# Linear attention and a gated feed-forward layer: the second tile's early work is queued behind the first x, and TensorE gets products of no use in the first attention's pauses

## The chip, the cores and the metric

The kernel runs on one core of one Trainium2 chip. A core has a matrix engine (TensorE, PE in the profile; PEld is its weight load), a vector engine (VectorE, DVE), a scalar engine (ScalarE, ACT), a general engine (GpSimd, POOL) and a queue that issues DMAs (SyncE, SP). They run side by side and wait for each other through semaphores; each takes its own instructions in order. The metric is the device time of one execution in microseconds; smaller is better.

## The reference

```
q_s = softmax of q over head_dim;  k_s = softmax of k over the sequence
kv  = k_s^T v                 # per batch and head, 64 x 64
x   = q_s kv                  # 8 batches x 576 tokens, 8 heads x 64 -> 4608 x 512
out = ((x @ w_a) * (x @ w_b)) @ w_out      # 512 -> 1536 -> 512
```

The weights w_a, w_b and w_out arrive as 64-bit floats; the kernel loads their words and makes 32-bit floats of them itself. Most products are made from a rounded operand ("hi") and its rest ("lo") in three passes.

## The kernel before, in words

The 4608 tokens are taken in nine tiles of 512. For every tile the attention makes x (four pairs of heads, g = 0 to 3), and the feed-forward runs over twelve blocks of 128 hidden columns, f = 0 to 11. Tile 0 uses plain products: `gate_first(f)` makes 24 products of 128 x 512 (two gates, four g, three passes each), `project_first(f)` four products in full float, two instructions each. The order on TensorE is gate 0, gate 1, projection 0, gate 2, projection 1, and so on. Tiles 1 to 8 use seven products per pair of blocks instead of eight (Strassen's scheme, operands B11, T2, T3, T1 and so on), and there TensorE is full.

Tile 0 is also the time in which the weights are made ready. `load_f(f)` loads two blocks of the gate weights (`raw`) and one of the output weights (`wo_raw`), 512 KB each. `convert_f(f)` (lines 517 to 520) rebuilds floats for each of the three in `to_float`: two copies on ScalarE (L97, L98), a shift on VectorE (L100), an addition on GpSimd (L101), a merge on VectorE (L102). For the two gate halves `convert_ab` then stores the floats (`dy`), splits them into hi and lo (`ws`: ScalarE L77, VectorE L80) and stores some of these (`dw`). `raw` tiles and the x tiles share one set of 11 buffers (tag `xo`).

The first attention (lines 525 to 540) runs, for each g: maximum and exponential of k (L236, L237), five transposes of it (L241), copies back (L242, L243), softmax of q (`q_soft_first` for even g, with sixteen small ScalarE instructions at L285; `q_soft` for odd g), the kv product (L249), its scaling and split (L254 to L257, L79, L80), four transposes of q (L316), their split (`qh`, `ql`), six or three x products (L333), and the split of x into hi and lo (L77, L80). `convert_f(0)` is traced after g = 1, `convert_f(1)` after g = 3.

In the loop over f that follows (lines 550 to 564), loads of later blocks, `convert_f(f + 2)`, one step of the second tile's attention (`attend()`, from f = 1 on: ten steps made of `s0` loads, `s1` softmax, `s2` products), the gate of f and the projection of f - 1 are traced in this order. `attention_tasks(1)` covers batch 1's four kv products and tile 1's four q.

The order in which the code is traced isn't the order of the queues: a planner at build time (line 685) orders each engine's instructions by an estimated timeline and takes up work early where an engine would be free and the buffers are there. `tc.issue_after(ins)` keeps the instructions of its block that run on `ins`'s engine behind `ins` in that engine's queue; it adds no wait between engines. Instructions of the block on other engines are not bound, DMA issues included.

Of the kernel before, what the change touches and what calls it, by code (L numbers as in the profile page):

```python
# [1 line left out]

# [5 lines left out]
F32 = mybir.dt.float32  # L8
# [5 lines left out]
ALU = mybir.AluOpType  # L14
# [15 lines left out]
def linear_attention_then_gated_ffn(  # L30
# [17 lines left out]
    nc = tc.nc  # L48
    B, NP, P, J, _, D = k.shape
# [3 lines left out]
    NF = 2 * NI  # L53
# [7 lines left out]
    ps = ctx.enter_context(tc.tile_pool(name="ps", bufs=1, space=bass.MemoryType.PSUM))  # L61
    dr = ctx.enter_context(tc.tile_pool(name="dr", bufs=1, space=bass.MemoryType.DRAM))

    ident = const.tile([P, P], F32, name="ident")
# [4 lines left out]
    mask = const.tile([P, P], F32, name="mask")  # L69
# [4 lines left out]
    def split(hi, lo, src, hi_engine="act"):  # L74

        if hi_engine == "act":
            nc.scalar.copy(out=hi, in_=src)  # L77
        else:
            nc.vector.tensor_copy(out=hi, in_=src)  # L79
        nc.vector.tensor_tensor(out=lo, in0=src, in1=hi.bitcast(F32), op=ALU.subtract)  # L80


    wo = {}
# [1 line left out]
    def to_float(raw):  # L85

        top = raw.bitcast(F32).rearrange("p (n t) -> p n t", t=2)[:, :, 1]
        low = raw.bitcast(U32).rearrange("p (n t) -> p n t", t=2)[:, :, 0]
        y = sb.tile([P, DM], F32, name="wy", bufs=8)
        r = sb.tile([P, DM], I32, name="wr", bufs=4)
        u = raw.bitcast(I32)[:, 0:DM]
        nc.scalar.activation(out=y, in_=top, func=AF.Copy, scale=2.0 ** -112)  # L97
        nc.scalar.activation(out=r, in_=low, func=AF.Copy, scale=2.0 ** -29)  # L98
        yi = y.bitcast(I32)
        nc.vector.tensor_single_scalar(u, yi, 3, op=ALU.logical_shift_left)  # L100
        nc.gpsimd.tensor_tensor(out=r, in0=u, in1=r, op=ALU.add)  # L101
        nc.vector.scalar_tensor_tensor(  # L102
            out=yi, in0=yi, scalar=-(2 ** 31), in1=r, op0=ALU.bitwise_and, op1=ALU.bitwise_or
        )
        return y
# [16 lines left out]
    def convert_wo(f):  # L122

        y = to_float(raws.pop((f, "o")))
        w = const.tile([P, 2, DM], F32R, name=f"wo{f}_w", tag=f"wo{f}")
        nc.sync.dma_start(out=w[:, 1].bitcast(F32), in_=y)
        wo[f] = w

    def split_wo(f):
        split(wo[f][:, 0], wo[f][:, 1], wo[f][:, 1].bitcast(F32))  # L130


    def ws_tile():
        return sb.tile([P, 2, 2, 2, P], F32R, name="ws", bufs=8)

    def split_w(y):
        w = ws_tile()
        yv = y.rearrange("p (n c f) -> p n c f", n=2, c=2)
        split(w[:, :, 0], w[:, :, 1], yv)
        return w  # L140

    dw, dy = {}, {}
    blocks = {}
# [1 line left out]
    def convert_ab(f, half):  # L145

        i, r = divmod(f, 2)
        y = to_float(raws.pop((f, half)))
        dy[i, r, half] = dr.tile([P, DM], F32, name=f"dy{i}{r}{half}")
        nc.sync.dma_start(out=dy[i, r, half], in_=y)  # L150
        w = split_w(y)
        op = ((A11, A12), (None, A22))[r][half]
        if op is not None:
            put_w(i, op, w)
        blocks[f, half] = w

    def put_w(i, op, w):
        dw[i, op] = dr.tile([P, 2, 2, 2, P], F32R, name=f"dw{i}{op}")
        nc.sync.dma_start(out=dw[i, op].bitcast(F32), in_=w.bitcast(F32))
# [30 lines left out]
    def v_load(b, g, vt=None):  # L190
        if vt is None:
            vt = sb.tile([P, J, 2, D + 1], F32, name="vt")
        nc.sync.dma_start(out=vt, in_=v[b, g])
        return vt
# [37 lines left out]
    def kv_soft_t(kt, tags):  # L232

        kf = kt.rearrange("p j c -> p (j c)")
        mc = sb.tile([P, 1], F32, name="mc")
        nc.vector.tensor_reduce(out=mc, in_=kf, axis=AX.X, op=ALU.max, negate=True)  # L236
        nc.scalar.activation(out=kf, in_=kf, func=AF.Exp, bias=mc)  # L237
        pa = ps.tile([P, J - 1, P], F32, name="pka", tag=tags[0])
        pb = ps.tile([P, P], F32, name="pkb", tag=tags[1])
        for j in range(J):  # L240
            nc.tensor.transpose(pa[:, j] if j < J - 1 else pb, kt[:, j], ident)  # L241
        nc.scalar.copy(out=kt[:, 0:J - 1], in_=pa)  # L242
        nc.vector.tensor_copy(out=kt[:, J - 1], in_=pb)  # L243
        return kt.rearrange("p j (h d) -> p j h d", h=2)

    def kv_product(kt, vt, tag="at"):
        pk = ps.tile([P, 2, D + 1], F32, name="pk", tag=tag)
        for j in range(J):
            nc.tensor.matmul(  # L249
                pk, kt[:, j].rearrange("p h d -> p (h d)"), vt[:, j],  # L250
                start=(j == 0), stop=(j == J - 1),
            )
        den = sb.tile([P, 1], F32, name="den")
        nc.vector.tensor_scalar_add(den, pk[:, 0, D:D + 1], EPS)  # L254
        nc.vector.reciprocal(out=den, in_=den)
        kv = sb.tile([P, P], F32, name="kv", bufs=1)
        nc.vector.scalar_tensor_tensor(  # L257
            out=kv.rearrange("p (h d) -> p h d", h=2), in0=pk[:, :, 0:D], scalar=den,
            in1=mask.rearrange("p (h d) -> p h d", h=2), op0=ALU.mult, op1=ALU.mult,
        )  # L260
        return kv
# [3 lines left out]
    def kv_split(b, g, kv):  # L265
        kvh = sb.tile([P, P], F32R, name=f"kvh{g}")
        kvl = sb.tile([P, P], F32R, name=f"kvl{g}")
        split(kvh, kvl, kv, "dve")
        kvs[b, g] = (kvh, kvl)
# [43 lines left out]
    def q_transpose(qt, tag="at"):  # L313
        pq = ps.tile([P, T], F32, name="pq", tag=tag)
        for j in range(TT):
            nc.tensor.transpose(  # L316
                pq[:, j * P:(j + 1) * P], qt[:, j].rearrange("p h d -> p (h d)"), ident
            )
        qh = sb.tile([P, T], F32R, name="qh", bufs=1)
        ql = sb.tile([P, T], F32R, name="ql", bufs=1)  # L320
        split(qh, ql, pq)
        return qh, ql

    def x_product(c, g, qhl, tag="at"):
        qh, ql = qhl
        t0 = c * T
        b0, b1 = t0 // S, (t0 + T - 1) // S
        n0 = min(T, (b0 + 1) * S - t0)
        px = ps.tile([P, T], F32, name="px", tag=tag)
        for b, s in ((b0, slice(0, n0)), (b1, slice(n0, T)))[:b1 - b0 + 1]:  # L330
            kvh, kvl = kvs[b, g]
            for i, (w, m) in enumerate(((kvh, qh), (kvh, ql), (kvl, qh))):
                nc.tensor.matmul(px[:, s], w, m[:, s], start=(i == 0), stop=(i == 2))  # L333
        return px


    def xo_tile(shape):
        return sb.tile(shape, F32R, name="xo", bufs=11)
# [168 lines left out]
    for g in range(NP):  # L507
        kt = const.tile([P, J, P], F32, name=f"kt_first{g}", tag=f"wo{NF - 1 - g}")
        vt = const.tile([P, J, 2, D + 1], F32, name=f"vt_first{g}", tag=f"wo{NF - 5 - g}")
# [3 lines left out]
        q_load(0, g, qt)  # L513
        v_load(0, g, vt)
    x0 = []

    def convert_f(f):
        convert_ab(f, 0)
        convert_ab(f, 1)
        convert_wo(f)  # L520

    for f in range(2):
# [2 lines left out]
    for g in range(NP):  # L525
        kt, vt, qt = first[g]
        odd = g % 2
        kt = kv_soft_t(kt, (("at", "k0"), ("k1", "k2"))[odd])
        if odd:
            q_soft(qt, True)  # L530
        else:
            q_soft_first(qt)
        kv_split(0, g, kv_product(kt, vt, ("po0", "po1")[odd]))
        qhl = q_transpose(qt, ("at", "k1")[odd])
        px = x_product(0, g, qhl, ("po2", "po3")[odd])
        x = xo_tile([P, 2, T])
        split(x[:, 0], x[:, 1], px)
        x0.append(x)
        if odd:
            convert_f(g // 2)  # L540


    early = (B11, T2, T3, T1)
# [2 lines left out]
    sy = {}  # L546
    attend = Spread(attention_tasks(1), 10)
    po = [ps.tile([P, DM], F32, name=f"po{t}") for t in range(TT)]
    pending = None
    for f in range(NF):  # L550
        for n in range(2, 4) if f == 0 else (f + 3,):
            if n < NF:
                last_load = load_f(n)
        if f + 2 < NF:
            convert_f(f + 2)
        if f:
            attend()
        if f == NF - 1:
            sy[0] = sums(0)
            x_operands(xfs[1], early + late, xo)  # L560
        ghl = gate_first(f, x0)
        if pending is not None:
            project_first(*pending, po)
        pending = (f, ghl)
# [11 lines left out]
    for c in range(1, NCH):  # L576
        more = c + 1 < NCH
        attend = Spread(attention_tasks(c + 1) if more else [], 3 * NI - 3)
        po = None
        x, xo = xo, {}  # L580
        for i in range(NI):
            def operand(op):
                if c > 1:
                    return get_w(i, op)
                if op in (A11, A12, A22):
                    return get_w(i, op)
                w = split_w(sy[i][op])
                put_w(i, op, w)
                return w

# [98 lines left out]
```

## Time and profile before

| | |
|---|---|
| median of 3 runs | 996.82 us (996.42 to 997.51) |
| the profiled execution | 995.74 us, of which span 993.3 us |
| busy: PE, DVE, ACT, POOL | 962.1, 654.0, 333.5, 114.2 us |
| mean granted clock of TensorE | 0.991 |

The span runs from the first to the last instruction; what is left of the profiled execution's time lies around it. All times in the rows below are counted from the span's start. A row of the timeline has the start, the duration, the engine, the line of the code, the instruction, what it writes and reads, how many were merged, and in brackets the idle time ahead of it and what ended it. Busy shares are averages over stages with different limits: tile 0, with its attention and conversions, takes the first 170 us or so, and the eight other tiles the rest.

### The profile page before, as it was taken

How to read it: one execution, taken by the hardware profiler on the slowest of the kernel's cores; microseconds unless marked ns; L12 is line 12 of the kernel's file. 1: busy time of each engine (PE TensorE's matmuls, PEld its weight loads, DVE VectorE, ACT ScalarE, POOL GpSimd, SP SyncE). 2: the span in 40 equal slices, each digit the busy share in tenths (PEclk: the TensorE clock that was granted, in tenths of full speed). 3: DMA queues.
4: the chain of work that ended last, by engine and by line, in shares of the span. 5: the costliest groups of instructions: out<-in, count | busy, mean ns of one | idle time of the engine just before them, and what ended most of it. 6: DMA issues, size and time to landing. Idle time of an engine off the chain costs nothing.

```text
span 993.3 us, 16580 instructions
## 1 busy us (share of the span) xinstructions
PE 962.1 (97%) x6276; PEld 866.0 (87%) x6276; DVE 654.0 (66%) x1280; ACT 333.5 (34%) x667; POOL 114.2 (11%) x96
## 2 busy tenths in 40 slices
PE   4889999999999999999999999999999999999998
PEld 4667666999989999999999999999999999999996
DVE  7797887887787774677468656865577555353433
ACT  7666675332342322233223212322233232121111
POOL 3344345440000000000000000000000000000000
PEclk9799998999999999999999999999999999999999
DMA  9599858978777587866796679767867676767761
GB/s 345 216 413 401 336 213 282 384 276 294 239 272 270 212 292 270 292 220 240 239 331 228 229 249 325 257 219 245 296 221 250 211 274 216 251 238 271 252 207 50
DMA packets 84605, 261.35 MB, mean 263 GB/s; under 512 B 9392, under 2 KB 9520, under 8 KB 84528
## 3 DMA queue, kind: packets, MB, share of 16 engines
q1 hardware_dynamic: 84528, 260.31, 73.8%
q8 instruction: 50, 0.82, 0.3%
q14 instruction: 27, 0.22, 0.1%
HBM read 219.38 MB, written 37.75 MB: 259 GB/s over the span
## 4 chain that ended last, share of the span: by engine, by line
PE 83%; DVE 4%; DMA 4%; issue 3%; ACT 2%; POOL 2%; SPq 0%; POOLq 0%; DVEq 0%; ACTq 0%
PE po L420 26%; PE ka L401 14%; PE kx L401 14%; PE kp L401 14%; PE ky L401 7%; PE pk L249 3%; PE px L333 2%; POOL wr L101 2%; PE pt L378 2%; PE po L410 1%; DMA wo_w<-wy 1%; PE pq L316 1%; DMA wo_raw<-in_w_out 1%; DVE ws L80 1%; DMA qt<-in_q 1%
## 5 line engine op out<-in xcount | busy, mean ns | idle before, releaser
L420 PE MATMUL po<-wo_w,gh 128*128 128x512 f32 x768 | 225.0, 394 | 1.0 <-ACT gh L77 1.0
L401 PE MATMUL kx<-xo,ws 128*128 128x256 f32 x1152 | 167.1, 285 | 0.0
L401 PE MATMUL ka<-xo,ws 128*128 128x256 f32 x1152 | 161.9, 285 | 0.2 <-ACT xo L77 0.2
L420 PEld LDWEIGHTS po<-wo_w,gh 128*128 128x128 f32 x768 | 138.4, 189 | 26.6 <-ACT gh L77 1.4
L401 PE MATMUL kp<-xo,ws 128*128 128x256 f32 x1152 | 157.4, 284 | 0.0
L401 PEld LDWEIGHTS kx<-xo,ws 128*128 128x128 f32 x1152 | 152.4, 191 | 4.0 <-ACT ws L77 0.2
L401 PEld LDWEIGHTS ka<-xo,ws 128*128 128x128 f32 x1152 | 151.3, 192 | 4.3 <-ACT xo L77 0.7
L401 PEld LDWEIGHTS kp<-xo,ws 128*128 128x128 f32 x1152 | 147.2, 191 | 1.6
L420 PE MATMUL po<-wo_w,gl 128*128 128x512 f32 x384 | 136.8, 397 | 0.0
L77 ACT CAST gh<-cc 128x512 fp32r<-128x512 f32 x96 | 58.7, 622 | 159.1 <-DVE cc L632 113.1
L631 DVE TENSOR_TENSOR cc<-kp,u 128x512 f32<-128x512 f32 x48 | 33.0, 687 | 82.3 <-PE kp L401 81.9
L420 PEld LDWEIGHTS po<-wo_w,gl 128*128 128x128 f32 x384 | 71.1, 189 | 14.8
L401 PE MATMUL ky<-xo,ws 128*128 128x256 f32 x576 | 80.1, 288 | 1.0 <-ACT xo L77 1.0
L378 PE MATMUL pt<-xo,ws 128*128 128x512 f32 x288 | 74.1, 406 | 3.9 <-ACT ga L385 3.2
L401 PEld LDWEIGHTS ky<-xo,ws 128*128 128x128 f32 x576 | 73.8, 194 | 1.6 <-ACT xo L77 1.4
L80 DVE TENSOR_TENSOR gl<-cc,gh 128x512 fp32r<-128x512 f32 x96 | 68.0, 714 | 10.1 <-ACT gh L77 10.1
L622 ACT COPY cc<-kx 128x256 f32<-128x256 f32 x48 | 17.9, 372 | 168.3 <-PE kx L401 162.9
L621 DVE TENSOR_TENSOR cc<-kp,u 128x512 f32<-128x512 f32 x48 | 33.0, 688 | 62.2 <-PE kp L401 61.9
L378 PEld LDWEIGHTS pt<-xo,ws 128*128 128x128 f32 x288 | 53.3, 188 | 20.3 <-ACT ga L385 4.6
L217 POOL PARTITION_ALL_REDUCE mx<-m x20 | 14.7, 733 | 475.1 <-DVE m L203 434.8
L410 PE MATMUL po<-wo_w,ga 128*128 128x512 f32 x96 | 43.5, 592 | 0.0
L635 DVE TENSOR_TENSOR cc<-ka,u 128x512 f32<-128x512 f32 x48 | 32.9, 685 | 15.4 <-PE ka L401 15.2
(119 smaller groups left out, 1211.0 us busy)
## 6 DMA issues: line engine op xcount, KB each, us to landing
ws<-dw SPq DMA_DIRECT2D x312, 512.0 KB, 4.7
dw<-ws SPq DMA_DIRECT2D x42, 512.0 KB, 4.7
raw<-in_w_ab SPq DMA_DIRECT2D x24, 512.0 KB, 7.9
out<-ot SPq DMA_DIRECT2D x36, 256.0 KB, 4.1
vt<-in_v SPq DMA_DIRECT2D x28, 325.0 KB, 6.1
qt<-in_q SPq DMA_DIRECT2D x32, 256.0 KB, 4.0
kt<-in_k SPq DMA_DIRECT2D x24, 320.0 KB, 4.6
wo_raw<-in_w_out SPq DMA_DIRECT2D x12, 512.0 KB, 8.1
```

The source lines that it names most:

```text
L77: nc.scalar.copy(out=hi, in_=src)
L80: nc.vector.tensor_tensor(out=lo, in0=src, in1=hi.bitcast(F32), op=ALU.subtract)
L101: nc.gpsimd.tensor_tensor(out=r, in0=u, in1=r, op=ALU.add)
L249: nc.tensor.matmul(pk, kt[:, j].rearrange("p h d -> p (h d)"), vt[:, j], start=(j == 0), stop=(j == J - 1),)
L333: nc.tensor.matmul(px[:, s], w, m[:, s], start=(i == 0), stop=(i == 2))
L378: nc.tensor.matmul(pt, w[:, wp], x[g][:, xp], start=(i == 0), stop=(i == 3 * NP - 1))
L401: nc.tensor.matmul(pt[:, n], w[:, n, wp, c], x[:, xp, c], start=(first and n == 0 and i == 0), stop=(i == 5), skip_group_check=True,)
L410: nc.tensor.matmul(po[t], g[:, t * P:(t + 1) * P], wo[f][:, 1].bitcast(F32), start=(f == 0), stop=(f == NF - 1),)
L420: nc.tensor.matmul(po[t], a[:, ts], wo[f][:, w], start=(f == 0 and i == 0), stop=(f == NF - 1 and i == 2),)
L621: nc.vector.tensor_tensor(out=cc[:, 3], in0=kp, in1=u3, op=ALU.add)
L631: nc.vector.tensor_tensor(out=cc[:, 1], in0=kp, in1=u2, op=ALU.add)
L635: nc.vector.tensor_tensor(out=cc[:, 2], in0=ka, in1=u2, op=ALU.add)
```

## The change

Four things are done. The names are those of the code.

- `convert_ab(0, ...)` stays after g = 1. `convert_wo(0)` and `convert_f(1)` are traced after the first attention, with their ScalarE and VectorE instructions queued behind the split of the last x (`behind(last_x)`).
- The second tile's attention begins at f = 2 instead of f = 1; its ScalarE and VectorE instructions at f are queued behind the ws split of block f + 1 (`done`).
- TensorE gets products of `mask` with itself (128 x 128, full float, result in `pw`, read by nobody): 14 ahead of the first k transposes, 6 behind each g's k transposes, which the kv product follows, 6 behind each g's q transposes, which the x products follow.
- `pw` has PSUM bank `po3`; so the x products of all g use bank `po2`, where odd g had `po3`.

```diff
     def split(hi, lo, src, hi_engine="act"):
...
-            nc.scalar.copy(out=hi, in_=src)
+            a = nc.scalar.copy(out=hi, in_=src)
...
+        return a, b
+
+    @contextmanager
+    def behind(pair):
+
+        with tc.issue_after(pair[0].ins), tc.issue_after(pair[1].ins):
+            yield
+
+    pw = ps.tile([P, P], F32, name="pw", tag="po3")
+
+    def warm(n, after=None):
+        with ExitStack() as pinned:
+            if after is not None:
+                pinned.enter_context(tc.issue_after(after.ins))
+            for _ in range(n):
+                after = nc.tensor.matmul(pw, mask, mask, start=True, stop=True)
+        return after
...
+    lastpe["warm"] = warm(14)
+
+    done = []
 
     def convert_f(f):
         convert_ab(f, 0)
-        convert_ab(f, 1)
+        done.append(convert_ab(f, 1))
         convert_wo(f)
...
-        kt = kv_soft_t(kt, (("at", "k0"), ("k1", "k2"))[odd])
+        with tc.issue_after(lastpe["warm"].ins):
+            kt = kv_soft_t(kt, (("at", "k0"), ("k1", "k2"))[odd])
+        w1 = warm(6, lastpe["kt"])
         if odd:
             q_soft(qt, True)
         else:
             q_soft_first(qt)
-        kv_split(0, g, kv_product(kt, vt, ("po0", "po1")[odd]))
+        with tc.issue_after(w1.ins):
+            kv_split(0, g, kv_product(kt, vt, ("po0", "po1")[odd]))
         qhl = q_transpose(qt, ("at", "k1")[odd])
-        px = x_product(0, g, qhl, ("po2", "po3")[odd])
+        w1 = warm(6, lastpe["pq"])
+        with tc.issue_after(w1.ins):
+            px = x_product(0, g, qhl, "po2")
         x = xo_tile([P, 2, T])
-        split(x[:, 0], x[:, 1], px)
+        last_x = split(x[:, 0], x[:, 1], px)
         x0.append(x)
-        if odd:
-            convert_f(g // 2)
+        if g == 1:
+            convert_ab(0, 0)
+            done.append(convert_ab(0, 1))
+
+    with behind(last_x):
+        convert_wo(0)
+        convert_f(1)
...
-        if f:
-            attend()
+        if f > 1:
+            with behind(done[min(f + 1, NF - 1)]):
+                attend()
```

`split_w` and `convert_ab` now return the pair of instructions that `split` returns; `lastpe` keeps the last transpose or product of each kind.

More of the change, by code (lines that the diff above doesn't have):

```diff
@@ L1 @@
-from contextlib import ExitStack
+from contextlib import ExitStack, contextmanager
 import concourse.bass as bass
@@ L76, in split @@
         if hi_engine == "act":
-            nc.scalar.copy(out=hi, in_=src)
+            a = nc.scalar.copy(out=hi, in_=src)
         else:
-            nc.vector.tensor_copy(out=hi, in_=src)
-        nc.vector.tensor_tensor(out=lo, in0=src, in1=hi.bitcast(F32), op=ALU.subtract)
+            a = nc.vector.tensor_copy(out=hi, in_=src)
+        b = nc.vector.tensor_tensor(out=lo, in0=src, in1=hi.bitcast(F32), op=ALU.subtract)
+        return a, b
[11 more added lines that the diff above has]
+        return after
+    lastpe = {}
     wo = {}
@@ L138, in split_w @@
         yv = y.rearrange("p (n c f) -> p n c f", n=2, c=2)
-        split(w[:, :, 0], w[:, :, 1], yv)
-        return w
+        return w, split(w[:, :, 0], w[:, :, 1], yv)
     dw, dy = {}, {}
@@ L150, in convert_ab @@
         nc.sync.dma_start(out=dy[i, r, half], in_=y)
-        w = split_w(y)
+        w, done = split_w(y)
         op = ((A11, A12), (None, A22))[r][half]
@@ L155, in convert_ab @@
         blocks[f, half] = w
+        return done
     def put_w(i, op, w):
@@ L240, in kv_soft_t @@
         for j in range(J):
-            nc.tensor.transpose(pa[:, j] if j < J - 1 else pb, kt[:, j], ident)
+            lastpe["kt"] = nc.tensor.transpose(pa[:, j] if j < J - 1 else pb, kt[:, j], ident)
         nc.scalar.copy(out=kt[:, 0:J - 1], in_=pa)
@@ L248, in kv_product @@
         for j in range(J):
-            nc.tensor.matmul(
+            lastpe["pk"] = nc.tensor.matmul(
                 pk, kt[:, j].rearrange("p h d -> p (h d)"), vt[:, j],
@@ L315, in q_transpose @@
         for j in range(TT):
-            nc.tensor.transpose(
+            lastpe["pq"] = nc.tensor.transpose(
                 pq[:, j * P:(j + 1) * P], qt[:, j].rearrange("p h d -> p (h d)"), ident
@@ L332, in x_product @@
             for i, (w, m) in enumerate(((kvh, qh), (kvh, ql), (kvl, qh))):
-                nc.tensor.matmul(px[:, s], w, m[:, s], start=(i == 0), stop=(i == 2))
+                lastpe["px"] = nc.tensor.matmul(px[:, s], w, m[:, s], start=(i == 0), stop=(i == 2))
         return px
@@ L586, in operand @@
                     return get_w(i, op)
-                w = split_w(sy[i][op])
+                w, _ = split_w(sy[i][op])
                 put_w(i, op, w)
```

## The prediction

> **What bounds the kernel now.** I read the stretches first, since the page's shares mix stages. Columns: stretch, its length, busy us (instructions) of PE, PEld, DVE, ACT, POOL, granted clock, DMA share, GB/s.
>
> ```profile
> 0.00:20.00 20.00, 10.40 (x43) 9.23 (x44) 12.56 (x35) 15.10 (x47) 4.96 (x12) 1.00 0.91 333
> 20.00:47.00 27.00, 19.73 (x87) 15.15 (x85) 23.70 (x50) 20.60 (x60) 10.96 (x9) 0.81 0.64 238
> 47.00:80.00 33.00, 30.04 (x121) 20.82 (x120) 25.89 (x38) 21.41 (x39) 15.16 (x10) 1.00 1.02 405
> 80.00:120.00 40.00, 39.06 (x161) 27.86 (x160) 32.44 (x59) 24.61 (x44) 18.70 (x13) 1.00 0.98 388
> 120.00:162.00 42.00, 41.77 (x165) 28.39 (x164) 32.79 (x48) 26.36 (x70) 22.72 (x17) 1.00 0.58 207
> 162.00:172.00 10.00, 7.54 (x26) 4.39 (x25) 9.27 (x16) 6.92 (x14) 1.73 (x2) 0.82 0.98 336
> 200.00:990.00 790.00, 785.60 (x5484) 733.27 (x5483) 492.13 (x992) 209.09 (x383) 27.06 (x28) 1.00 0.71 248
> ```
>
> From 200 us on TensorE stands still for 4.4 of 790 us. No line of the change touches the products there, so time can come or go only before about 172. There the stretches 47 to 162 are nearly full of TensorE work too (110.9 of 115 us), with VectorE 79% busy (91.1 of 115). In 20 to 47 it is the other way: VectorE is full (23.70 of 27), TensorE not, and DMA is at 0.64. So I ask what sets the moment at which TensorE gets going. The timeline of the queues answers.
>
> ```profile
> 46.29 0.69 DVE L80 TENSOR_TENSOR xo<-px,xo 128x512 fp32r<-128x512 f32 x1
> 44.67 2.67 PE L378 MATMUL pt<-xo,ws 128*128 128x512 f32 x11
> 50.74 5.74 PE L378 MATMUL pt<-xo,ws 128*128 128x512 f32 x24 [0.77 <-ACT ga L385]
> 56.32 3.59 PE L410 MATMUL po<-wo_w,ga 128*128 128x512 f32 x8
> 71.00 3.00 PE L378 MATMUL pt<-xo,ws 128*128 128x512 f32 x12 [2.19 <-ACT ga L385]
> 156.60 3.59 PE L410 MATMUL po<-wo_w,ga 128*128 128x512 f32 x8
> ```
>
> The fourth x of the first token tile is complete at 46.29 + 0.69 = 46.98. I call this moment X. Only then can block 0's gate (24 products) end, and block 1's starts at 50.74. From there each of the 12 blocks costs 5.74 + 3.59 = 9.3 us of TensorE: eleven of them make 102.6 us, and the stretch to 162 has little room beside them. So **X is the lever**: what X gains, the end gains, if the conversions that feed the gates can follow.
>
> **What the change does to X.** Between 20 and 47 VectorE works on three things: the first attention, the conversions of blocks 0 and 1, and the second tile's attention, taken up early. The groups of 0 to 47 on VectorE (columns: busy us, mean ns, idle before):
>
> ```profile
> L102 DVE SCALAR_TENSOR_TENSOR wy<-wy,wr 128x512 int32<-128x512 int32 x6 | 5.3, 884 | 0.0
> L80 DVE TENSOR_TENSOR ws<-wy,ws 128x512 fp32r<-128x512 f32 x4 | 4.8, 1223 | 0.0
> L100 DVE TENSOR_SCALAR raw<-wy 128x512 int32<-128x512 int32 x4 | 2.5, 634 | 0.0
> L100 DVE TENSOR_SCALAR wo_raw<-wy 128x512 int32<-128x512 int32 x2 | 0.8, 413 | 0.0
> L236 DVE TENSOR_REDUCE mc<-kt 128x1 f32<-128x640 f32 x3 | 2.4, 807 | 1.2 <-DMA kt<-in_kt 1.2
> L282 DVE TENSOR_REDUCE qst<-qt 128x8 f32<-128x512 f32 x2 | 1.4, 676 | 0.0
> L257 DVE SCALAR_TENSOR_TENSOR kv<-pk,den,mask 128x128 f32<-128x128 f32 x5 | 1.7, 344 | 0.0
> L79 DVE CAST kvh<-kv 128x128 fp32r<-128x128 f32 x5 | 1.8, 352 | 0.0
> L80 DVE TENSOR_TENSOR kvl<-kv,kvh 128x128 fp32r<-128x128 f32 x5 | 1.4, 288 | 0.0
> ```
>
> *Conversions that move behind the fourth x* (`convert_wo(0)`, `convert_f(1)`: four of the six, two of the four ws splits): 4/6 x 5.3 + 2/4 x 4.8 + 2/4 x 2.5 + 0.8 = 8.0 us. *Second attention that moves behind block 3's conversion*: 2.4 + 1.4, one kv of five (1.7 + 1.8 + 1.4)/5 = 1.0, and for its small copies and reciprocals about as much again as L282's row, 1.5 (an estimate): 6.3 us. Together 14.3 us leave VectorE's queue ahead of X, of 23.70.
>
> ScalarE loses as much, and there it is on the chain of waits itself:
>
> ```profile
> 38.21 2.82 ACT qt L285 x17
> L285 ACT ACTIVATE qt<-qt,qst 128x64 f32<-128x64 f32 x16 | 5.3, 341 | 0.0
> 44.87 0.59 ACT L77 CAST xo<-px 128x512 fp32r<-128x512 f32 x1 [1.87 <-PE px L333]
> ```
>
> Sixteen exponentials of the second tile's q stand ahead of the third and fourth x. ScalarE isn't the next bound: it was busy 20.60 us of 27, and these 5.3 and the four conversions leave it. What is late next is the last head's own chain (cast of q, its rest, three products, cast of x, its rest), in which VectorE waits: ScalarE's cast of x alone waited 1.87 us for TensorE. I take off 1.3 us for that. **Term A: X moves from 47.0 to about 34, -13 us**; bounds -10 (the chain leaves VectorE idle twice as long as now, 3.3 us more) and -14.3.
>
> *The raw weights.* They must move too. On SP's queue:
>
> ```profile
> 42.29 0.33 SPq L229 DMA_DIRECT2D kt<-in_kt  x1
> 43.14 0.90 SPq L114 DMA_DIRECT2D raw<-in_w_ab  x2
> ```
>
> Blocks 2 and 3 are loaded from 43.14, right behind a k load of the second attention that had waited, and between the casts of the third and fourth x, with which the raws share 11 buffers (four x, eight raws: one too many). Then DMA is full (1.02 from 47 to 80). In the change those k loads are traced after the raws of block 5, and the x come 13 us earlier. I let the raws move with X, at no cost: DMA's share of 0.64 is the room. If they don't, block 2's gate stays at its time and all is lost: a rival.
>
> *The products of no use.* 14 at the start, 6 behind each head's k transposes and 6 behind each q transposes: 48 in the heads. None stands in the trace; the nearest rows are kv products of nearly the same shape, ten instructions for five products:
>
> ```profile
> 1.12 0.33 POOL L72 MEMSET mask<- 64x64 f32 x2
> 5.84 1.11 PE L241 MATMUL pka<-ident,kt_first 128*128 128x128 f32 x4 [5.84 <-ACT kt_first L237]
> 8.99 2.53 PE L249 MATMUL pk<-vt_first,kt_first 128*128 128x130 f32 x10 [1.83 <-ACT kt_first L242]
> 48.68 1.28 PE L249 MATMUL pk<-vt,kt 128*128 128x130 f32 x10
> L378 PE MATMUL pt<-xo,ws 128*128 128x512 f32 x20 | 5.9, 415 | 0.7 <-DVE xo L80 0.7
> L249 PE MATMUL pk<-vt,kt 128*128 128x130 f32 x10 | 2.4, 424 | 0.0
> L241 PE MATMUL pka<-ident,kt 128*128 128x128 f32 x8 | 1.7, 349 | 0.2 <-ACT kt L242 0.2
> L241 PE MATMUL pkb<-ident,kt 128*128 128x128 f32 x2 | 0.8, 404 | 3.0 <-DVE kt L243 1.9 <-DVE ql L80 1.1
> ```
>
> The same work takes 2.53 us early and 1.28 later, so the array runs at half rate in the first attention, though the granted clock of 0 to 20 reads 1.00 (the durations decide). One product of no use costs 0.26 us at full and 0.51 at half rate; 48 cost 12.3 or 24.3 us. The room from 5.84 (first transpose) to 34 is 28 us. The first attention's own TensorE work is the 30.1 us of 0 to 47 less 5.9, 2.4, 1.7 and 0.8 (the second tile's products and transposes, and the gate's) = 19.3, mostly at half rate, some 11 at full rate. 11 + 12.3 fits into 28; 19.3 + 24.3 doesn't. The 14 at the start run from about 1.5 us (mask set) and take 3.6 to 7.1, so to 8.6 at the latest; the first transposes begin at 5.84 now, but what follows them waits for a copy of ScalarE until 8.99, so these hide. Against delays of up to 1 us where a pause is shorter than six products stand faster products of the last head. **Term B: 0**, bounds -2 and +3 at full rate; half rate is a rival.
>
> Which rate? The early kv products ran at half rate while TensorE was busy about half of the time (10.40 of 20 us); from 47 on, where it is busy 91% and more, the same products run at full rate. With the products of no use it is nearly without pause, so I take full rate. The Trainium skill (TensorE: Matmul & The Clock Gate, Part 1) says that the array starts throttled, is released by about 3.4 us of sustained activity and falls back after an idle window of that length. By that rule the 14 products release the clock and the sum stays; by the early rows alone, as if the stage set the rate, the price would be that of rival 4.
>
> *Block 1 behind X.* Its conversion now starts at X. Three conversions pass GpSimd in 64.39 - 57.52 = 6.9 us:
>
> ```profile
> 57.52 1.61 POOL L101 TENSOR_TENSOR wr<-raw,wr 128x512 int32<-128x512 int32 x1 [1.22 <-issue]
> 64.39 1.66 POOL L101 TENSOR_TENSOR wr<-raw,wr 128x512 int32<-128x512 int32 x1 [0.36 <-DVE raw L100]
> ```
>
> So its second half is ready at X + 8, where its gate began at X + 3.8 before; half of its products need only the first half. **Term C: +2**, bounds 0 (now, too, TensorE waits 2.19 at 71.0 for block 3, and the delay runs into such gaps) and +4.
>
> *Second attention later.* Its 6.3 us of VectorE join a stretch where VectorE is 79 to 81% busy. **Term D: +2.5**, bounds 0 (all in idle time) and +6.3 (none).
>
> **Sum:** -13 + 0 + 2 + 2.5 = -8.5 us. On the profiled execution's 995.74 (span 993.3 and 2.4 around it) that is 987.2; the median of the runs, 996.82, lies 1.1 higher, so **988.3**.
>
> **Rivals.**
>
> 1. *VectorE, or the raws, bind after X.* VectorE has 114.8 us to do between 20 and 162 and is idle 27. A gain of 8.5 asks for 86% busy, of 3 for 83%, against 81% now. For it: DMA at 1.02 and VectorE never over 81% after 47. Against it: 20 to 47 shows 88%, and part of the idle time lies before the raws of 43.14 land. Gain 1 to 5, 994.
>
> 2. *Only TensorE binds.* The deferred work vanishes in idle time: A alone, 13 to 14: 983.
>
> 3. *Slower: the second attention becomes the last to end.* It is nearly so now:
>
> ```profile
> 109.91 5.72 PE L378 MATMUL pt<-xo,ws 128*128 128x512 f32 x24
> 116.57 0.30 PE L333 MATMUL px<-qh,kvh 128*128 128x64 f32 x1 [0.94 <-DVE ql L80]
> 166.21 0.30 PE L333 MATMUL px<-qh,kvh 128*128 128x64 f32 x1 [0.72 <-DVE ql L80]
> ```
>
> Its first x product follows block 7's gate, ahead of which it is traced; its last comes at 166.21, after block 11's, though it is traced ahead of block 10's. The second tile's products wait for it. In the change each step is traced one block later and may not be taken up early. One block is 9.3 us. Up to 13/9.3 = 1.4 blocks more of delay are paid by A; at two blocks, 18.6 - 13 = +5.6, less the part that C and D already count: 1001. For it: this tail, with TensorE busy 7.54 of 10 us. Against it: ten steps still fit into ten blocks, and work of the third tile stands in this stretch that can wait.
>
> 4. *The products of no use run at half rate.* 43.6 us against room for 28: X at 50, +3, with C 1002. For it: the early rows now. Against it: the rate from 47 on, where TensorE has as few pauses.
>
> 5. *The change doesn't do what it says*: the orders already hold, or the raws stay at 43: 996.8.
>
> **Chances.** Forecast (gain 5 to 12) 0.52; rival 1 0.16; rival 2 0.12; rival 3 0.12; rival 4 0.05; rival 5 0.03. About 2 us (0.2%) is what a measurement of this kernel can tell from no change. Faster: 0.52 + 0.12 + three quarters of rival 1 = 0.76; within: a quarter of it and rival 5, 0.07; slower 0.17. Range 981 to 997: the forecast, rivals 1 and 5 and most of rival 2; left out are 3 and 4.
>
> **What would show it.** A: the fourth x's L80 ends at 32 to 37, with no L285 on qt ahead of it. Raws of block 2 issued before 36. B: kv products of heads 1 to 3 at 1.3 us instead of 2.5. C: block 1's gate starts 4 to 8 us after X. D: VectorE over 82% from X to the end of the last project. The end: that project, at 156.60 now, at 146 to 150, and the last x product of the second tile not more than 8 us behind it. The prediction is wrong if X moves less than 8 us, or if that last product comes after 162.

## The result, and the profile after

The changed kernel takes 1025.38 us (median of 4 runs, 1023.73 to 1028.09), the kernel before 996.75 beside it: ratio 1.0291, 95% interval 1.0275 to 1.0307. It is 2.9% slower, where 988.3 was forecast. The profiled execution's span went from 993.3 to 1024.3 us.

The stretches after, in the columns of the prediction's first fence:

```profile
20.00:47.00 27.00, 19.49 (x124) 16.60 (x122) 21.00 (x37) 16.54 (x30) 10.25 (x8) 0.89 0.95 355
47.00:80.00 33.00, 31.17 (x106) 20.94 (x107) 28.55 (x39) 20.33 (x35) 17.75 (x11) 0.93 0.99 374
80.00:120.00 40.00, 37.86 (x142) 24.95 (x141) 30.06 (x49) 26.09 (x58) 17.71 (x12) 1.00 0.78 285
120.00:162.00 42.00, 38.89 (x154) 25.72 (x153) 28.89 (x46) 20.38 (x47) 21.99 (x15) 1.00 0.62 214
172.00:200.00 28.00, 14.16 (x45) 10.24 (x46) 16.77 (x32) 13.72 (x48) 7.54 (x6) 0.50 0.34 120
```

Two things are to be seen. Between 47 and 162 TensorE does a little less than before (107.9 us of 115, before 110.9), although x was ready earlier. And there is a new stretch, 172 to 200, where no engine is busy for more than 60% of the time and the granted clock is 0.50; before, the second tile filled TensorE there:

```profile
172.00:200.00 28.00, 28.00 (x201) 26.92 (x201) 25.07 (x48) 9.41 (x17) 12.93 (x8) 0.94 1.01 385
```

TensorE's timeline after the change shows what it waits for:

```profile
163.28 3.70 PE L431 MATMUL po<-wo_w,ga 128*128 128x512 f32 x8
166.82 0.60 PE L337 MATMUL pq<-ident,qt 128*128 128x128 f32 x4
170.81 0.90 PE L337 MATMUL pq<-ident,qt 128*128 128x128 f32 x4 [0.72 <-issue]
183.62 1.12 PE L337 MATMUL pq<-ident,qt 128*128 128x128 f32 x4 [2.40 <-POOL qt L312]
187.41 0.42 PE L354 MATMUL px<-qh,kvh 128*128 128x64 f32 x1 [2.68 <-DVE ql L80]
190.26 1.08 PE L337 MATMUL pq<-ident,qt 128*128 128x128 f32 x4 [0.72 <-issue]
192.80 0.42 PE L354 MATMUL px<-qh,kvh 128*128 128x64 f32 x1 [1.46 <-DVE ql L80]
198.18 0.58 PE L422 MATMUL ky<-xo,ws 128*128 128x256 f32 x1 [1.02 <-ACT xo L77]
```

The last projection of tile 0 ends at 167.0. All four q heads of the second tile (`pq`, then `px`) come behind it, one after the other, with little beside them: only the second tile's first product `kx`, whose operand takes two heads, runs in between. The operand of its second product `ky` is made from all four heads, and `ky` starts at 198.2. Before, it started at 169.5:

```profile
169.48 0.58 PE L401 MATMUL ky<-xo,ws 128*128 128x256 f32 x1 [1.05 <-ACT xo L77]
```

Of the 31.0 us that the span grew, 28.7 lie ahead of this product. The rest, 2.3, lies in the 826 us behind it.

Why are the heads so late? VectorE's maxima of k, the SP queue's k loads (from the second on) and the kv products of the second attention, in order:

```profile
68.43 0.81 DVE L257 TENSOR_REDUCE mc<-kt 128x1 f32<-128x640 f32 x1
79.83 0.81 DVE L257 TENSOR_REDUCE mc<-kt 128x1 f32<-128x640 f32 x1
119.56 0.81 DVE L257 TENSOR_REDUCE mc<-kt 128x1 f32<-128x640 f32 x1
143.94 0.81 DVE L257 TENSOR_REDUCE mc<-kt 128x1 f32<-128x640 f32 x1
```

```profile
16.00 0.33 SPq L250 DMA_DIRECT2D kt<-in_kt  x1
94.24 0.38 SPq L250 DMA_DIRECT2D kt<-in_kt  x1
135.93 0.41 SPq L250 DMA_DIRECT2D kt<-in_kt  x1
```

```profile
89.07 1.28 PE L270 MATMUL pk<-vt,kt 128*128 128x130 f32 x10
128.71 1.39 PE L270 MATMUL pk<-vt,kt 128*128 128x130 f32 x10 [0.32 <-DVE kt L264]
154.44 1.28 PE L270 MATMUL pk<-vt,kt 128*128 128x130 f32 x10
161.86 1.36 PE L270 MATMUL pk<-vt,kt 128*128 128x130 f32 x10 [1.33 <-DVE kv L278]
```

Read them as one chain. There are two k buffers: the third load (94.24) follows the first kv product (89.07), the fourth (135.93) the second (128.71). The second product waits for a copy out of the transposes (L264): they share the PSUM bank `at`, in the order traced, and so do the q heads. Before, the third load went out at 42.3, and the first two maxima were these:

```profile
28.27 0.81 DVE L236 TENSOR_REDUCE mc<-kt 128x1 f32<-128x640 f32 x1
32.35 0.79 DVE L236 TENSOR_REDUCE mc<-kt 128x1 f32<-128x640 f32 x1
```

Now the three moments are 68.4, 79.8 and 94.2. What was done early, in front of the fourth x, was the head start of a serial chain.

### The profile page after: what moved, and what is told of

Its sections match the earlier page's. It is cut to its first block, busy times and chain, and to the rows that moved or that the text cites. A ratio compares the mean times of both kernels' runs of the same rounds, so it can differ in the third digit from the quotient of the medians.

```text
span 1024.3 us, 16840 instructions
## 1 busy us (share of the span) xinstructions
PE 979.6 (96%) x6400; PEld 879.6 (86%) x6400; DVE 660.1 (64%) x1280; ACT 334.4 (33%) x667; POOL 114.4 (11%) x96
## 4 chain that ended last, share of the span: by engine, by line
PE 77%; DVE 5%; DMA 2%; ACT 2%; issue 1%; POOL 0%; SPq 0%; DVEq 0%; POOLq 0%; ACTq 0%
PE po L441 25%; PE ka L422 13%; PE kp L422 13%; PE kx L422 13%; PE ky L422 7%; PE pk L270 3%; PE px L354 2%; PE pq L337 1%; DVE ws L80 1%; DMA qt<-in_q 1%; DMA ws_y<-dy 1%; ACT qt L306 0%; POOL ws_y L201 0%; PE po L431 0%; DVE wy L123 0%
## 5 line engine op out<-in xcount | busy, mean ns | idle before, releaser
L80 DVE TENSOR_TENSOR gl<-cc,gh 128x512 fp32r<-128x512 f32 x96 | 66.8, 701 | 10.5 <-ACT gh L77 10.5
```

The costliest lines, as they stand in the source:

```text
L80: b = nc.vector.tensor_tensor(out=lo, in0=src, in1=hi.bitcast(F32), op=ALU.subtract)
```

## The experiments

The moments in the table are read from each run's timeline, in us: x is the end of the fourth x's rest, gate 1 and gate 11 the end of the multiplication behind these gates (`ga`), px the start of the second tile's last x product, ky the second tile's first `ky`. They come from one profiled execution of each run; that of e3 took 1002.3 us, 4 us more than the median of its runs. The last two columns are the median and the ratio to the kernel before, run beside it, with its interval.

```
run                        x   gate 1  gate 11    px     ky     median   ratio
before                   47.0   60.0   157.6   166.2  169.5     996.8
after                    36.0   58.8   163.2   192.8  198.2    1025.4   1.0291 (1.0275-1.0307)
e1_no_products           34.4   57.6   159.3   189.8  194.8    1017.4   1.0200 (1.0185-1.0215)
e2_products_alone        45.5   58.5   156.0   164.7  168.0     996.9   1.0000 (0.9990-1.0011)
e3_attend_as_before      40.3   61.5   161.1   166.3  169.9     998.2   1.0026 (1.0008-1.0045)
e4_convert_as_before     40.7   51.2   148.9   188.7  193.7    1022.8   1.0258 (1.0243-1.0273)
e5_late_unbound          38.3   59.7   156.3   167.0  171.1    1000.6   1.0035 (1.0019-1.0052)
e6_two_steps             35.5   58.3   164.0   190.0  195.4    1024.0   1.0278 (1.0261-1.0295)
e7_three_buffers         35.6   57.0   158.7   173.1  178.3    1012.8   1.0163 (1.0143-1.0184)
e8_behind_x_only         41.1   58.4   159.4   178.2  182.4    1007.7   1.0115 (1.0100-1.0130)
e9_before_buffers        48.4   65.5   168.3   151.8  168.3     995.7   0.9990 (0.9979-1.0001)
e10_before_buffers_bank  49.9   66.4   171.7   152.0  171.8     996.6   0.9992 (0.9979-1.0006)
e11_x_buffers_bank       41.2   57.4   168.3   154.1  168.3    1000.9   1.0037 (1.0023-1.0051)
e12_bound_buffers        41.8   51.6   157.6   169.5  177.9    1009.5   1.0118 (1.0097-1.0139)
f1_before_relief         45.2   54.1   163.5   172.5  176.4    1007.9   1.0118 (1.0091-1.0145)
f2_x_early_relief        38.2   61.4   166.3   172.6  175.9    1006.4   1.0104 (1.0083-1.0125)
f4_before_copy_rest      43.5   54.9   152.5   157.6  161.2     992.8   0.9961 (0.9948-0.9974)
f5_x_early_copy_rest     36.8   57.2   154.9   159.8  163.3     994.9   0.9977 (0.9960-0.9993)
```

### Which part of the change costs the time: e1 to e4

Theory 1: the second attention, late and tied to the conversions, ends last. Theory 2: the products of no use crowd TensorE. Theory 3: conversions behind the fourth x starve the gates. e1 takes the products out of the changed kernel:

```diff
-    lastpe["warm"] = warm(14)
...
-        w1 = warm(6, lastpe["kt"])
...
-        w1 = warm(6, lastpe["pq"])
-        with tc.issue_after(w1.ins):
-            px = x_product(0, g, qhl, "po2")
+        px = x_product(0, g, qhl, ("po2", "po3")[odd])
```

> The changed kernel without the 62 products of no use, and with the x products of odd heads back in bank po3. Theory 1 (the second tile's attention, started late and tied to the conversions, ends last; the products cost nothing): 1019 to 1031 us, its last x product still after 190 us. Theory 2 (the products of no use crowd TensorE and delay the first attention and all behind it): 994 to 1005. Theory 3 (conversions queued behind the fourth x starve the gates): 1019 to 1031.

e2 puts them alone into the kernel before; it is the changed kernel with these two places as they were (e3 has only the second, e4 only the first of them):

```diff
-        if g == 1:
-            convert_ab(0, 0)
-            done.append(convert_ab(0, 1))
-
-    with behind(last_x):
-        convert_wo(0)
-        convert_f(1)
+        if odd:
+            convert_f(g // 2)
...
-        if f > 1:
-            with behind(done[min(f + 1, NF - 1)]):
-                attend()
+        if f:
+            attend()
```

> The kernel before with the 62 products and bank po2 for all heads, nothing else moved. Theory 1: 992 to 1000 us. Theory 2: above 1012. Theory 3: 992 to 1000.

> The changed kernel with the second tile's attention as it was: from block 1 on, its instructions bound to nothing; products and conversions stay as changed. Theory 1: 984 to 1000 us, the last x product of the second tile before 170 us. Theory 2: above 1015. Theory 3: above 1012, with block 11's gate no earlier than in the changed kernel (149.9 us).

> The changed kernel with block 0's and 1's conversions traced where they were and bound to nothing; the second attention stays late and bound, the products stay. Theory 1: 1013 to 1035 us, last x product after 185 us. Theory 2: above 1015, but with the first attention as slow as in the changed kernel. Theory 3: 992 to 1003.

Of the three that take one part out (e1, e3, e4) only e3 brings the time back, to 998.2; with the attention late (e1, e4) ky stays near 194. Theory 1 holds, though e1 ended 1.6 us below its range, with the last x product at 189.8 and not after 190. (The 149.9 in e3's expectation is the start of that gate; the table has the ends.) The products cost nothing alone (e2). In the changed kernel they stand, together with the PSUM bank that they take, for 8.0 us, which no theory had: of the 8.6 us between the two profiled spans 3.4 lie ahead of ky, and 5.2 behind it, where no such product runs. From ky to the end the spans of these runs differ by up to 12 us (820.9 in e1, 833.3 in e7) with the same products; the planner orders that stage anew in every build, and I could not tie the 5.2 to a part of the change.

e4 shows what the fourth x could have been worth. Conversions where they were, second attention out of the way: x at 40.7 and, unlike in e3, gate 1 early too.

```profile
40.05 0.69 DVE L80 TENSOR_TENSOR xo<-px,xo 128x512 fp32r<-128x512 f32 x1 [1.60 <-ACT xo L77]
50.53 0.68 DVE L407 TENSOR_TENSOR ga<-pt,ga 128x512 f32<-128x512 f32 x1
```

The same lines of e3, whose x comes at the same time:

```profile
39.59 0.68 DVE L80 TENSOR_TENSOR xo<-px,xo 128x512 fp32r<-128x512 f32 x1
60.84 0.68 DVE L407 TENSOR_TENSOR ga<-pt,ga 128x512 f32<-128x512 f32 x1
```

Both `ga` lines are the multiplication behind block 1's gate. With the conversions behind x it ends 21 us after x instead of 11. e3 and e4 differ in the attention too, but two pairs differ in the conversions alone and say the same: from e4 to the changed kernel x comes 4.7 us earlier and gate 1 7.6 later, from e2 to e3 x 5.2 earlier and gate 1 3.0 later. So **moving block 1's conversion behind x took back all that x gained**, already at gate 1.

An early gate 1 isn't an early end either. From gate 1 to gate 11 it is 97.6 us in the kernel before, 97.5 in e2, 97.7 in e4: ten blocks, near the 93 us of their own products. But this is no constant: in the changed kernel it is 104.4, and in the others 96.6 (e5) to 110.9 (e11). And in e4 gate 1 is 8.8 us early and ky 24.2 us late, behind the heads.

### What makes the second attention late: e5 to e8

e5 traces it from block 2 on but doesn't bind it; e6 traces two steps per block and binds them. Their edits stand ahead of the expectations.

```diff
         if f > 1:
-            with behind(done[min(f + 1, NF - 1)]):
-                attend()
+            attend()
```

> The changed kernel with the second attention still traced from block 2 on, but its instructions bound to nothing. If the binding to the conversions is what delays it: 994 to 1003 us, k maxima of the second tile taken up before 45 us. If the later start in the trace order is enough: 1012 to 1026, k maxima after 60 us.

```diff
-    attend = Spread(attention_tasks(1), 10)
+    attend = Spread(attention_tasks(1), 5)
```

> The changed kernel with two steps of the second attention per block (all ten traced from block 2 to 6), each bound as before. If the pace at which steps are traced and bound sets its end: 992 to 1008 us, last x product before 172 us. If its own chain through one PSUM bank and two buffers sets it: 1016 to 1028, last x product after 184 us.

Without the binding the maxima are at 25 and 27 us again and ky at 171.1: the binding is the cause, not the later tracing. Two steps per block change next to nothing (1024.0): the third maximum moves from 119.6 to 108.0, the fourth only from 143.9 to 140.8. So it isn't the pace at which steps are handed out. e7 gives the chain a third buffer (here the k tile; v and q alike):

```diff
-            kt = sb.tile([P, J, P], F32, name="kt")
+            kt = sb.tile([P, J, P], F32, name="kt", bufs=3)
```

> The changed kernel with three buffers instead of two for the k, v and q tiles of the later attentions. If the wait for a free buffer (third k load at 94.2 us, third q load at 171.5) lengthens the chain: 1005 to 1019 us, third k load before 30 us. If the pace alone sets it: 1021 to 1029.

```profile
13.57 0.33 SPq L250 DMA_DIRECT2D kt<-in_kt  x1
15.68 0.33 SPq L250 DMA_DIRECT2D kt<-in_kt  x1
18.26 0.33 SPq L250 DMA_DIRECT2D kt<-in_kt  x1
94.43 0.38 SPq L250 DMA_DIRECT2D kt<-in_kt  x1
```

The third load goes out at 18.26 instead of 94.24, and ky comes 19.9 us earlier; 7 of these are lost again behind ky, for a reason that stays open. At ky the hops over the buffers are the larger part of the delay, 19.9 of 28.7 us. e8 tries a middle way: conversions as before, no products of no use, attention from block 1 on, bound behind the fourth x alone.

```diff
         if f:
-            attend()
+            with behind(last_x):
+                attend()
```

> A combination: conversions as before, no products of no use, the second attention from block 1 on and bound only behind the split of the fourth x. If the fourth x may come 6 us earlier and the second attention still ends in time: 986 to 994 us, last gate before 152 us, last x product before 163 us. If VectorE's work after the fourth x takes it all back: 995 to 1000. If the second attention's chain, started 12 us later, ends last: 1001 to 1012.

```profile
14.91 0.33 SPq L249 DMA_DIRECT2D kt<-in_kt  x1
61.94 0.42 SPq L249 DMA_DIRECT2D kt<-in_kt  x1
94.94 0.38 SPq L249 DMA_DIRECT2D kt<-in_kt  x1
```

The third load, 19.6 us later than the 42.3 of the kernel before, becomes 12.9 us at ky: in the kernel before, too, the chain has no room to start later.

### Does a shorter chain make room: e9 to e12

e9 is the kernel before with three buffers, e10 adds a PSUM bank of its own for the second tile's x products, e11 and e12 put both on e8 and on a version that binds as the change does (conversions as before, no products of no use).

```diff
-                px = x_product(c, g, q_transpose(box["e"]))
+                px = x_product(c, g, q_transpose(box["e"]), "k2" if c == 1 else "at")
```

> The kernel before with three buffers instead of two for the k, v and q tiles of the later attentions, nothing else. If the second attention's chain is already as late as TensorE can bear (its last product at 166 us, after the last gate at 157.6): 985 to 994 us. If it has room in the kernel before: 995 to 998.

> The same, and the second tile's x products in the bank of the k transposes (k2) instead of the one that the q transposes use too. If the one bank holds back the q heads at the end: 2 to 6 us below the run with the buffers alone. If not: within 2 us of it.

> The combination of the run behind the fourth x (conversions as before, no products of no use, second attention bound only behind the fourth x, 1007.7 us) with three buffers and bank k2. If its 11 us were the chain's: 985 to 997 us, last x product before 168 us. If VectorE after the fourth x sets the end: above 1001.

> Conversions as before, no products of no use, the second attention late and bound as in the change, but with three buffers and bank k2. If the chain's hops over buffers and bank are the whole delay: 990 to 1003 us. If tying each step to a block's conversion delays it by itself: 1005 to 1016.

None of the hoped-for gains came: e9, e10 and e12 fell into their second ranges, e11 just below its second. The buffers do what they should: in e9 the last px is at 151.8, 14 us earlier. But gate 11 is 10.7 us later, and ky is where it was. The two streams of tile 0's time, attention and blocks, trade: e4 has gates 8.7 us earlier and heads 22.5 later, e9 the reverse, and the kernel before ends both within 8.6 us of each other. The bank gave nothing (996.6 against 995.7). With both, the bound version is still 12.6 us above the kernel before (e12), where e4 is 26.3 above. How much of that difference the buffers and the bank make isn't shown, since e12 also lacks the products of no use, which stand for 8.0 us between the changed kernel and e1.

### Which engine the trade runs over: f1, f2, f4 and f5

24 of VectorE's instructions in the conversions, the rests of the `ws` split, go to GpSimd (f1 on the kernel before, f2 on e3), or ScalarE writes a copy in their place (f4, f5; there the rests are left out).

```diff
-        nc.vector.tensor_tensor(out=lo, in0=src, in1=hi.bitcast(F32), op=ALU.subtract)
+        (nc.gpsimd if lo_engine == "pool" else nc.vector).tensor_tensor(
+            out=lo, in0=src, in1=hi.bitcast(F32), op=ALU.subtract)
```

> The kernel before, with the rest of the gate weights' split (one of VectorE's instructions per half block in the conversions, 24 in all) on GpSimd. If VectorE's sum of work sets when the second tile can start: 984 to 993 us. If it doesn't, or if GpSimd's part of the conversion is the slower partner: 996 to 1006.

> The same move on the kernel with the early fourth x and the second attention as before (998.2 us). If VectorE's sum takes the early x back: 984 to 993 us. If the conversions' order or GpSimd takes it back: 996 to 1008.

> The kernel before, with the same 24 subtractions left out: ScalarE copies the unrounded weights in their place, so the rests are not what the reference has. Some 22 us of VectorE time with its stalls go. If VectorE's sum is the bound: 980 to 990 us. If TensorE's own products leave no room: 993 to 997.

> The same copies in place of the subtractions (rests not the reference's) on the kernel with the early fourth x. If VectorE takes the early x back: 976 to 988 us, below the same edit on the kernel before by the 5 us that its x is earlier. If the order of the conversions takes it back: within 3 us of that run.

GpSimd made it slower by 11 us in f1, beyond both of its ranges, and by 8 in f2 against e3, though VectorE's busy time from 47 to 149 fell from 83.08 to 74.63 in f1. The same 102 us in f4, and in the kernel before (second fence):

```profile
47.00:149.00 102.00, 101.46 (x398) 71.10 (x399) 70.16 (x115) 78.22 (x164) 54.50 (x38) 1.00 0.90 351
```

```profile
47.00:149.00 102.00, 97.88 (x388) 67.72 (x387) 83.08 (x133) 67.77 (x143) 46.55 (x32) 1.00 0.87 340
```

13 us less of VectorE gave 8.3 us at ky and 4.3 at the end, and then TensorE was full (101.46 of 102). So the stage gains from such a relief, but there are only some 4 us of TensorE's idle time in this stretch to win (f4 lies between its two ranges). The copy takes away VectorE's work and a hop between engines at once, since the rest had to wait for ScalarE's cast; f4 doesn't tell which of the two counts. And the early x is worth nothing even then: f5's x is 6.7 us earlier than f4's, and its gate 1 2.3 us later. No version of this study beat the kernel before with the reference's values by more than its interval.

## Why the prediction was wrong, point by point

**X is the lever: the step that failed first.** Term A itself was right: x went from 47.0 to 36.0 (-11 for -13, and 32 to 37 had been named), block 2's raw weights were issued at 26.48 instead of 43.14. But the end doesn't follow x. What x gained went no further than block 1's gate, which moved by 1.2 us (Term C); in e3, with the second attention as it was, an x 6.7 us earlier gives 998.2. And in the changed kernel the end follows what the sum had priced as VectorE work alone (Term D): the last head of the second attention, at 192.8 instead of 166.2. That puts 28.7 of the 31.0 us ahead of `ky`.

**Term C was mis-sized and cancelled A.** +2 was forecast, with block 1's second half ready at X + 8 from GpSimd's pace of three conversions in 6.9 us. It was X + 13.7. Lines of VectorE's queue (others between them are left out) show why GpSimd's pace isn't the price:

```profile
35.31 0.69 DVE L80 TENSOR_TENSOR xo<-px,xo 128x512 fp32r<-128x512 f32 x1 [1.68 <-ACT xo L77]
40.45 0.68 DVE L123 SCALAR_TENSOR_TENSOR wy<-wy,wr 128x512 int32<-128x512 int32 x1
41.06 1.50 DVE L121 TENSOR_SCALAR wo_raw<-wy 128x512 int32<-128x512 int32 x1
43.08 1.39 DVE L123 SCALAR_TENSOR_TENSOR wy<-wy,wr 128x512 int32<-128x512 int32 x1
44.39 0.41 DVE L121 TENSOR_SCALAR raw<-wy 128x512 int32<-128x512 int32 x1
45.33 1.76 DVE L80 TENSOR_TENSOR ws<-wy,ws 128x512 fp32r<-128x512 f32 x1
47.95 1.77 DVE L80 TENSOR_TENSOR ws<-wy,ws 128x512 fp32r<-128x512 f32 x1
```

The first half is merged by 41.1, yet its rest (L80) starts at 45.33: shifts and merges of the next conversions are queued ahead of it. A conversion is a relay over three engines, each with its own queue: from the start of GpSimd's addition (38.59) to the end of its rest (47.09) the first half took 8.5 us, of which the addition was 1.66. The gate's first product came at X + 7.0, as forecast, but twenty of the 24 waited for that rest:

```profile
42.99 2.07 PE L399 MATMUL pt<-xo,ws 128*128 128x512 f32 x4 [4.95 <-ACT ws L77]
47.14 6.89 PE L399 MATMUL pt<-xo,ws 128*128 128x512 f32 x20 [2.07 <-DVE ws L80]
```

ScalarE's copy of the gate then started at 57.05, 3.0 us after the last product, behind conversions in its queue. (The 2.19 us at 71.0 in the prediction are by their row a wait for such a copy, `ga`, not for block 3's conversion itself.) Block 1's gate ended 22.8 us after x, before 13.0: the term was +9.8.

**Term D was the wrong question.** The second attention's 6.3 us of VectorE were asked for room in idle time, and there was room: VectorE was busy 78% of the time from x to the end of the last projection, not over 82%. But it isn't an amount of work but a chain: two k buffers, one PSUM bank, four kv and four q heads in order. Its start moved by 40 us (first maximum 28.3 to 68.4), and the end of the chain by 26.6 (px).

**Rival 3 is what happened**, with a chance of 0.12. Its place was right, its size not. It named two causes, that each step is traced one block later and that it may not be taken up early, and priced the first: 9.3 us per block, 1001 in all. e5 and e6 show that tracing and pace don't matter. The delay comes from the second, the binding, and most of it through the buffers (e7); and all of it shows at the end, as A had nothing left to pay it with.

**Term B and rival 4.** The 14 at the start took 6.08 us, between the 3.6 and 7.1 of the forecast and so nearer to half rate. From there on the products ran at full rate, as taken: the next six took 1.50 us, and the first kv product 1.39 instead of 2.53:

```profile
1.50 6.08 PE L98 MATMUL pw<-mask 128*128 128x128 f32 x28 [1.50 <-POOL mask L72]
7.97 1.50 PE L98 MATMUL pw<-mask 128*128 128x128 f32 x12
11.95 1.39 PE L270 MATMUL pk<-vt_first,kt_first 128*128 128x130 f32 x10 [0.83 <-ACT kt_first L263]
```

Alone they cost nothing, 0 for 0. That they would lengthen the changed kernel by 8 us was not foreseen, and 5.2 of it stays open.

**Rival 1** (VectorE binds after x) was right in that the early x is lost between x and the blocks (e3: 998.2); f5, where the early x gives nothing although 24 of VectorE's instructions are gone, speaks for the order of the conversions as its cause and against VectorE's sum. Rivals 2 and 5 didn't occur: x and the raw weights did move, and TensorE wasn't the only bound. The range ended at 997, because the sum took each delay as one that idle time mostly absorbs.

## What to carry to other kernels

When work is moved off a critical point, ask what it starts: a step that is cheap in busy time can be the head of a serial chain over a few buffers, and then its start is worth as much as the point that it was moved away from. Follow the consumer that needs the last of several inputs (here block 1's gate: x and converted weights) before calling one input the lever. Where two streams end close to each other, as here, moving work from one to the other gained nothing in any of these runs.

## What the hardware showed unexpectedly

Waits cost twice. In 172 to 200, with pauses of 0.7 to 2.7 us between short bursts, the granted clock fell to 0.50, and the same x product took 0.72 us instead of 0.45:

```profile
169.23 0.45 PE L354 MATMUL px<-qh,kvh 128*128 128x448 f32 x1
188.07 0.72 PE L354 MATMUL px<-qh,kvh 128*128 128x448 f32 x1
```

The Trainium skill (TensorE: Matmul & The Clock Gate, Part 1) has the array fall back after an idle window of about 3.4 us. Here the granted clock is 1.00 from 170 to 171 us and 0.51 from 171 to 172, and no pause since 162 was longer than 1.45 us by then (1.9 between products, if the transposes aren't counted). So in this trace shorter pauses were enough.

Instructions moved from VectorE to GpSimd took twice as long there. In f1, between 47 and 149, GpSimd took 1.39 us for each rest that VectorE does in 0.68 when undisturbed:

```profile
L80 POOL TENSOR_TENSOR ws<-wy,ws 128x512 fp32r<-128x512 f32 x19 | 26.3, 1387 | 11.2 <-ACT ws L77 11.2
```

The same VectorE instruction takes 0.68 or 1.76 us within one kernel, and the trace shows when. The two rests at 45.33 and 47.95 in the changed kernel (shown under Term C) started while an addition ran on GpSimd, and ended 0.56 us after it:

```profile
44.88 1.65 POOL L122 TENSOR_TENSOR wr<-raw,wr 128x512 int32<-128x512 int32 x1 [0.96 <-DVE raw L121]
47.50 1.66 POOL L122 TENSOR_TENSOR wr<-raw,wr 128x512 int32<-128x512 int32 x1 [0.97 <-DVE raw L121]
```

Of the 24 such rests in the conversions, the 11 that started 0.08 us or more into a GpSimd instruction ended 0.54 to 0.56 us after it; the other 13 took 0.67 to 0.69 us. The Trainium skill (SBUF — State Buffer, "SBUF: two separate sides") says that a VectorE instruction with two SBUF inputs and a GpSimd instruction that reads SBUF take a shared port pair in turns, for whole instructions. The trace agrees with that.
